# Attention and a gated spatial MLP on one core: part 2 of a written-out order is tied to part 1 on VectorE, ScalarE and the SyncE queue, and the order itself is another

## The chip, the cores and the metric

The kernel runs on one core of one Trainium2 chip. The metric is the device time of one execution in microseconds, and the median of several executions. A core has engines with one instruction queue each: TensorE (PE in the profile, its weight loads PEld), VectorE (DVE), ScalarE (ACT), GpSimd (POOL) and SyncE (SP), which here only issues DMAs. Across engines, an instruction waits on semaphores for what it reads or overwrites.

## The reference

For batch B=4, heads H=4, sequence S=1088, head width D=32 and R=8 features, linear attention with quadratic features, and a gated MLP whose gate mixes positions (w_sg is 1088 x 1088):

```python
def phi(x):
    a = np.einsum('rd,bhsd->bhsr', S1, x)
    b = np.einsum('rd,bhsd->bhsr', S2, x)
    return np.einsum('bhsi,bhsj->bhsij', a, b).reshape(*x.shape[:-1], r * r)
q_p, k_p = phi(q), phi(k)
kv = np.einsum('bhsf,bhsd->bhfd', k_p, v)
z = np.sum(k_p, axis=2)
x = np.einsum('bhsf,bhfd->bhsd', q_p, kv) / (np.einsum('bhsf,bhf->bhs', q_p, z)[..., None] + 1e-06)
...
h = x @ w_in                                  # x: (4, 1088, 128), w_in: (128, 1024)
h = gelu_tanh(h)
u, v = h[..., :512], h[..., 512:]
v_n = (v - mu) / np.sqrt(var + 1e-06) * g_ln  # mean and variance over the last axis
v_s = np.einsum('ts,bsd->btd', w_sg, v_n) + b_sg[None, :, None]
out = x + (u * v_s) @ w_out
```

## The kernel before

Matrices are held as a high word in TensorE's fp32r format and a low word that holds the rest, so that a product is three matmuls (high x high, low x high, high x low). The positions are split into chunks of 420, 420 and 248 columns (CH), the 512 channels of the gate into four blocks of 128. Much of the work by position is done on 9 tiles of 128 positions.

**Tasks and the order.** Nothing is issued while the program is described. `add` and `step` record tasks (an engine, a function, what it reads, writes, takes and frees), 1963 of them. `ORDER` is a list of task numbers, written out, which fixes the order of all work; `plan.run()` replays it and hands out buffers: three banks of PSUM called ps, five buffers gt, three u, two gh, two gl.

**Two parts.** The list is issued in two parts (L1301 on). `staging` names the last tasks that need the pool `stage` (the splitting of the weights w_in and w_out, lines L453 to L471 on VectorE, among them); the first part ends behind the last of these. Then the pool is closed, the pools `x1` and `gate` are opened, and the second part is issued. Each part stands under its own `tc.manual_schedule()`, which keeps the listed order on each engine within the part. Nothing in the program says how the two parts stand to each other on an engine, apart from the dependencies of data and buffers.

**What stands around the cut**, at about 65 us:
- `unit` (L744 to L748): u of one block and chunk, three matmuls into a bank of ps (L746, L747, L748); ScalarE's gelu (L752) frees the bank.
- The first product with w_sg of batch 0 is accumulated in banks that are called `ps`, `po` and `pz` (L680, L1241, L1243). `evac` (L762 on VectorE) adds the bias and writes gt, and the bank is free. `gate` multiplies by u (L776), splits into words (L777, L778), and three matmuls L783 to L785 multiply by w_out.
- `combine` (L865 to L895): makes differences of blocks of w_sg, with which later products take fewer matmuls, in eight rounds. A round loads pieces of w_sg (L879, L881: tmp<-in_w), subtracts on VectorE (L884 to L887), splits (L889, L890 on ScalarE; L891, L892 on VectorE) and stores to DRAM (L894: td<-tmp). The next round's loads overwrite tmp, so they wait for the stores. `combine` also copies words of w_sg as they are (L868: td<-w_h, L870: td<-w_l); the low words of w_sg are made on GpSimd (L700).
- `attention` (L905 to L1042) of the next batch: its scores of q are formed chunk by chunk (L956, L957 words of q, three matmuls L961 to L963), spread by a round trip through DRAM (`fill`, L969 to L975, two loads), multiplied and split (L978 to L980), and multiplied with kv (L987 to L989).
- In the first 25 us the attention of batch 0: products L605 on VectorE of the two halves of the features, L565 to L567 the division, then the transposes L574 on TensorE.

The products of batch 3 (`group` L831 to L833, `tail` L842 and L843, words L806 and L807) run the same way behind 300 us.

Of the kernel before, what the change touches and what calls it, by code (L numbers as in the profile page):

```python
# [20 lines left out]
SP = NT * P  # L21
# [170 lines left out]
def tile_kernel(ctx: ExitStack, tc: tile.TileContext, qd, kd, vd, sd, wd, bd, wind, gd, woutd, identd, outd):  # L192
# [1121 lines left out]
    with tc.manual_schedule():  # L1314
        for i in seq[cut:]:
            issue(plan.tasks[i])
# [36 lines left out]
```

## Time and profile before

| | |
|---|---|
| median of 3 timed runs | 337.05 us (336.94 to 337.54) |
| the profiled execution | 336.07 us |
| its span, first to last instruction | 333.9 us |
| TensorE busy (matmuls), weight loads | 325.9 us (98%), 313.9 us (94%) |
| VectorE busy, 595 instructions | 268.1 us (80%) |
| ScalarE busy, 525 instructions | 219.9 us (66%) |
| GpSimd busy | 55.3 us (17%) |
| granted TensorE clock, mean | 1.000 |

The profile shows one execution. A busy time is the time in which an engine carried out at least one instruction; matmuls overlap each other in the rows, so how long one holds TensorE is read from the distance between the starts of successive ones. The remainder between the span and the time of the execution lies around the first and last instruction.

### The profile page before, as it was taken

What the parts mean: (1) busy time and instruction counts of PE and PEld (TensorE: products, weight loads), DVE (VectorE), ACT (ScalarE), POOL (GpSimd) and SP (SyncE); (2) the same over time, 40 slices, a digit from 0 to 9 for tenths busy, and PEclk for the clock granted to TensorE, in tenths of its full rate; (3) what the DMA queues carried; (4) which work ended last, traced back from release to release, by engine and by line L of the source; (5) the groups of instructions that cost most, each with busy time, mean ns of one, the idle gap of its engine ahead of it and who ended that gap; (6) DMA issues with size and microseconds to landing.
All of it is one profiled execution on the core that took longest, in us unless ns stands there. A gap on an engine that the chain in (4) does not pass through costs nothing.

```text
span 333.9 us, 5891 instructions
## 1 busy us (share of the span) xinstructions
PE 325.9 (98%) x2000; PEld 313.9 (94%) x2000; DVE 268.1 (80%) x595; ACT 219.9 (66%) x525; POOL 55.3 (17%) x130
## 2 busy tenths in 40 slices
PE   7999999979999999999999999999999999999995
PEld 7998899969999999999999999999999999999995
DVE  3898989889986798997985588898964697589394
ACT  6578972646999886636789793746799953342240
POOL 2696781000004300000003300000004400000000
PEclk9999999999999999999999999999999999999999
DMA  7998244647668777882464428563434037115802
GB/s 237 369 397 297 66 111 143 221 128 186 189 176 271 214 170 202 282 283 82 113 215 161 165 75 219 153 214 113 136 106 174 2 101 258 71 52 157 255 3 70
DMA packets 43855, 57.06 MB, mean 171 GB/s; under 512 B 4209, under 2 KB 41137, under 8 KB 43825
## 3 DMA queue, kind: packets, MB, share of 16 engines
q1 hardware_dynamic: 43680, 56.62, 54.3%
q8 instruction: 16, 0.26, 0.3%
q14 instruction: 15, 0.11, 0.1%
q10 hardware_dynamic: 144, 0.06, 0.1%
HBM read 46.73 MB, written 9.95 MB: 170 GB/s over the span
## 4 chain that ended last, share of the span: by engine, by line
PE 76%; DVE 12%; DMA 4%; ACT 4%; issue 2%; SPq 1%; DVEq 0%; POOL 0%; ACTq 0%; POOLq 0%
PE pz L831 14%; PE pz L832 14%; PE pz L833 14%; PE ps L938 3%; PE po L783 2%; PE po L785 2%; PE po L784 2%; PE pz L842 2%; PE pz L843 2%; DMA tmp<-in_w 2%; PE ps L746 2%; PE ps L747 2%; PE ps L748 2%; PE ps L1020 2%; PE ps L1022 2%
## 5 line engine op out<-in xcount | busy, mean ns | idle before, releaser
L831 PE MATMUL pz<-w_h,ar 128*128 128x420 f32 (+1 forms) x288 | 94.3, 327 | 0.1
L832 PE MATMUL pz<-w_h,ar 128*128 128x420 f32 (+1 forms) x288 | 93.2, 324 | 0.0
L833 PE MATMUL pz<-w_l,ar 128*128 128x420 f32 (+1 forms) x288 | 93.1, 323 | 0.0
L831 PEld LDWEIGHTS pz<-w_h,ar 128*128 128x128 f32 x288 | 54.2, 188 | 1.7 <-DVE gt L762 0.7
L832 PEld LDWEIGHTS pz<-w_h,ar 128*128 128x128 f32 x288 | 54.2, 188 | 0.8
L833 PEld LDWEIGHTS pz<-w_l,ar 128*128 128x128 f32 x288 | 54.2, 188 | 0.6
L806 ACT CAST ar<-vn 128x512 fp32r<-128x512 f32 x40 | 24.5, 617 | 22.1 <-PE pz L833 19.4
L777 ACT CAST gh<-gt 128x420 fp32r<-128x420 f32 (+1 forms) x47 | 23.1, 494 | 17.0 <-DVE gt L776 13.0
L752 ACT ACTIVATE u<-ps 128x420 f32<-128x420 f32 (+1 forms) x48 | 22.4, 468 | 15.5 <-DVE gt L776 6.7
L778 DVE TENSOR_TENSOR gl<-gt,gh 128x420 fp32r<-128x420 f32 (+1 forms) x47 | 24.7, 531 | 6.5 <-ACT gh L777 6.3
L807 DVE TENSOR_TENSOR ar<-vn,ar 128x512 fp32r<-128x512 f32 x40 | 27.2, 685 | 0.8 <-ACT ar L806 0.6
L320 ACT ACTIVATE vn<-vn,st 128x512 f32<-128x512 f32 x33 | 25.9, 811 | 1.4 <-POOL st L314 1.4
L776 DVE TENSOR_TENSOR gt<-gt,u 128x420 f32<-128x420 f32 (+1 forms) x47 | 24.7, 529 | 0.2
L762 DVE SCALAR_TENSOR_TENSOR gt<-pz,g_col,b_bc 128x420 f32<-128x420 f32 (+1 forms) x31 | 17.7, 572 | 6.5 <-PE pz L843 4.2
L700 POOL TENSOR_TENSOR w_l<-w_f,w_h 128x420 fp32r<-128x420 f32 (+1 forms) x21 | 21.6, 1055 | 3.2 <-DVE sp_wi_e L457 2.8
L1032 ACT ACTIVATE kp<-vn,st 128x512 bf16<-128x512 f32 x27 | 19.5, 722 | 0.3
L746 PE MATMUL ps<-x_h,win_h 128*128 128x420 f32 (+1 forms) x48 | 16.1, 335 | 2.1 <-DVE gt L762 2.1
L303 POOL TENSOR_TENSOR st<-st 128x4 f32<-128x4 f32 (+2 forms) x8 | 2.4, 302 | 93.2 <-DVE st L285 93.2
L1029 ACT ACTIVATE vn<-ps 128x512 f32<-128x512 f32 x27 | 15.9, 590 | 1.4 <-PE ps L1022 1.3
L747 PE MATMUL ps<-x_h,win_l 128*128 128x420 f32 (+1 forms) x48 | 15.7, 328 | 0.0
L748 PE MATMUL ps<-x_l,win_h 128*128 128x420 f32 (+1 forms) x48 | 15.7, 327 | 0.0
L783 PE MATMUL po<-gh,wout_h 128*128 128x420 f32 (+1 forms) x47 | 15.6, 333 | 0.0
(303 smaller groups left out, 821.0 us busy)
## 6 DMA issues: line engine op xcount, KB each, us to landing
w_l<-td SPq DMA_DIRECT2D x52, 210.0 KB
w_h<-td SPq DMA_DIRECT2D x26, 420.0 KB
td<-tmp SPq DMA_DIRECT2D x16, 315.0 KB
w_f<-in_w SPq DMA_DIRECT2D x9, 544.0 KB
eb<-dq SPq DMA_DIRECT2D x12, 182.0 KB
ea<-dq SPq DMA_DIRECT2D x12, 182.0 KB
vn<-in_k SPq DMA_DIRECT2D x3, 576.0 KB
tmp<-in_w SPq DMA_DIRECT2D x16, 105.0 KB
```

Source lines behind the costliest of these rows:

```text
L320: A.activation(self.vn(t), self.vn(t), AF.Identity, bias=self.nm[:, t : t + 1], scale=self.rs[:, t : t + 1])
L746: mm(o, lhsT=win_h[:, ws], rhs=xh[:, cs], start=True, stop=False)
L747: mm(o, lhsT=win_l[:, ws], rhs=xh[:, cs], start=False, stop=False)
L752: add("A", 0.02 + ap(cw), lambda: A.activation(utt[plan.got[u]][:, :cw], ps(k)[:, :cw], AF.Gelu_apprx_tanh), r=[k], take={u: "u"}, free=[k ...
L776: add("V", dv(cw), lambda: V.tensor_mul(gt(k)[:, :cw], gt(k)[:, :cw], utt[plan.got[u]][:, :cw]), r=[u], w=[k], free=[u], port=1)
L777: add("A", ac(cw), lambda: A.copy(ght[plan.got[h]][:, :cw], gt(k)[:, :cw]), r=[k], take={h: "gh"})
L778: add("V", dv(cw), lambda: V.tensor_sub(glt[plan.got[l]][:, :cw], gt(k)[:, :cw], f32(ght[plan.got[h]][:, :cw])), r=[h, k], take={l: "gl"}, ...
L806: add("A", ac(n), lambda: A.copy(dst[:, 0], q()), r=r, w=[key])
L807: add("V", dv(n), lambda: V.tensor_sub(dst[:, 1], q(), f32(dst[:, 0])), r=r, w=[key], port=1)
L831: mm(o, lhsT=ar[e][:, 0, t], rhs=wh, start=first, stop=False, skip_group_check=True)
L832: mm(o, lhsT=ar[e][:, 1, t], rhs=wh, start=False, stop=False, skip_group_check=True)
L833: mm(o, lhsT=ar[e][:, 0, t], rhs=wl, start=False, stop=last, skip_group_check=True)
```

## The change

Three edits. The list `ORDER` is another one (the same tasks; 164 lines of numbers in the difference, of which the first pair is shown). `fill` hands back its two loads as a tuple; what it issues is the same. And `issue` remembers, while part 1 is issued, the last instruction of VectorE, of ScalarE and of the SyncE queue; in part 2, the first instruction of each of the three gets a dependency on it, of the kind that only the scheduler sees (NoSync, SCHED_ONLY: no semaphore, no instruction).

```diff
 ORDER = [
-    1, 2, 3, 4, 5, 11, 12, 6, 13, 14, 15, 16, 17, 18, 7, 50, 0, 51, 42, 8, 49, 48, 43, 9,
+    1, 2, 3, 4, 5, 11, 12, 6, 13, 14, 15, 16, 17, 18, 7, 45, 49, 8, 48, 0, 42, 46, 9, 51,
...
                 def fill(cw=cw, ci=ci, i=i, e=e):
                     o = here(e)[:, :, :cw]
-                    for p in range(2):
-                        if i:
-                            load(o[:, p], dq[ci][32 + 16 * p : 48 + 16 * p, :cw].unsqueeze(0).broadcast_to([R, 16, cw]))
-                        else:
-                            load(o[:, p], dq[ci][16 * p : 16 * p + 16, :cw].unsqueeze(1).broadcast_to([16, R, cw]))
+                    if i:
+                        return tuple(load(o[:, p], dq[ci][32 + 16 * p : 48 + 16 * p, :cw].unsqueeze(0).broadcast_to([R, 16, cw])) for p in range(2))
+                    return tuple(load(o[:, p], dq[ci][16 * p : 16 * p + 16, :cw].unsqueeze(1).broadcast_to([16, R, cw])) for p in range(2))
...
-    def issue(t):
+    last = {}
+
+    def issue(t, tie=False):
         ins = t["f"]()
+        if t["eng"] in ("V", "A", "SP"):
+            x = ins[0] if isinstance(ins, tuple) else ins
+            if tie and t["eng"] in last:
+                tc.add_manual_dep(x.ins, last.pop(t["eng"]).ins.name, mybir.DependencyInfo(mybir.DependencyClass.NoSync, mybir.DependencyReason.SCHED_ONLY), reason="order")
+            elif not tie:
+                last[t["eng"]] = ins[-1] if isinstance(ins, tuple) else ins
...
     with tc.manual_schedule():
         for i in seq[cut:]:
-            issue(plan.tasks[i])
+            issue(plan.tasks[i], True)
```

Behind `fill` the line numbers of the changed kernel are two lower, so L980 of before is L978 of after, and L995 is L993.

How the instructions stand is shown at three places, all on VectorE. The first is the end of part 1, at 65 to 72 us of the trace. The names sp_wo_ and wout belong to the splitting of w_out, which is part 1; tmp is combine's buffer; ar the words of the normalized v; gt the results of the evacuations; eb and qtl belong to the attention of batch 1. Before:

```order
L458 TENSOR_SCALAR sp_wo_g<-sp_wo_t 128x512
L884 TENSOR_TENSOR tmp<-tmp 128x210
L885 TENSOR_TENSOR tmp<-tmp 128x210
L807 TENSOR_TENSOR ar_92<-vn,ar_92 128x512
L470 TENSOR_TENSOR sp_wo_t<-sp_wo_t,wout_h 128x512
L459 SCALAR_TENSOR_TENSOR sp_wo_e<-sp_wo_e,sp_wo_g 128x512
L995 STREAM_TRANSPOSE r_521<-r_519 128x384
L471 TENSOR_TENSOR wout_l<-sp_wo_t,sp_wo_e 128x512
L998 TENSOR_SCALAR dr<-r_521 128x12
L999 RECIPROCAL dr<-dr 128x12
L886 TENSOR_TENSOR tmp<-tmp 128x210
L762 SCALAR_TENSOR_TENSOR gt_893<-ps_116,g_col,b_bc 128x248
```

After:

```order
L458 TENSOR_SCALAR sp_wo_g<-sp_wo_t 128x512
L978 TENSOR_TENSOR eb<-ea,r_839 128x2x364
L470 TENSOR_TENSOR sp_wo_t<-sp_wo_t,wout_h 128x512
L459 SCALAR_TENSOR_TENSOR sp_wo_e<-sp_wo_e,sp_wo_g 128x512
L957 TENSOR_TENSOR qtl<-qld,qth 128x364
L471 TENSOR_TENSOR wout_l<-sp_wo_t,sp_wo_e 128x512
L807 TENSOR_TENSOR ar_92<-vn,ar_92 128x512
L993 STREAM_TRANSPOSE r_707<-r_705 128x384
L762 SCALAR_TENSOR_TENSOR gt_893<-po_123,g_col,b_bc 128x248
L762 SCALAR_TENSOR_TENSOR gt_894<-pz_119,g_col,b_bc 128x420
L884 TENSOR_TENSOR tmp<-tmp 128x210
L762 SCALAR_TENSOR_TENSOR gt_895<-ps_118,g_col,b_bc 128x248
```

L884 and L885, operations of part 2, stood ahead of L807, L470, L459, L995 and L471 of part 1; they stand behind these now, and L884 behind two evacuations L762. The evacuation that ends the first piece (of 128 x 248, from a bank ps) is the one that ends the second. L980 (now L978) and the query's low word L957 (now L955), which stood ahead of L458, now stand behind it. The bank of that evacuation is used again on TensorE by a matmul L746: between the bank's last product and that matmul stood nine other matmuls, and now twenty.

The second place is in part 1, at 15 to 21 us: the attention of batch 0 and the splitting of w_in (sp_wi_). The names po, ps and pz are banks of PSUM. Before:

```order
L526 TENSOR_TENSOR sg_kvx<-pz_120,mask 128x2x32 x2
L528 TENSOR_TENSOR sg_kvx<-pz_120,mask 128x2 x2
L605 TENSOR_TENSOR vn<-po_122,ea 128x384
L459 SCALAR_TENSOR_TENSOR sp_wi_e<-sp_wi_e,sp_wi_g 128x512
L470 TENSOR_TENSOR sp_wi_t<-sp_wi_t,win_h 128x512
L565 TENSOR_SCALAR den_0_349<-pz_119 128x12
L566 RECIPROCAL den_0_349<-den_0_349 128x12
L567 TENSOR_TENSOR r_104<-pz_119,den_0_349 128x384
L605 TENSOR_TENSOR vn<-po_122,eb 128x384
L605 TENSOR_TENSOR vn<-ps_118,ea 128x384
```

After:

```order
L605 TENSOR_TENSOR vn<-pz_119,eb 128x384
L458 TENSOR_SCALAR sp_wi_g<-sp_wi_t 128x512
L605 TENSOR_TENSOR vn<-po_122,ea 128x384
L526 TENSOR_TENSOR sg_kvx<-pz_120,mask 128x2x32 x2
L528 TENSOR_TENSOR sg_kvx<-pz_120,mask 128x2 x2
L459 SCALAR_TENSOR_TENSOR sp_wi_e<-sp_wi_e,sp_wi_g 128x512
L605 TENSOR_TENSOR vn<-ps_118,ea 128x384
L470 TENSOR_TENSOR sp_wi_t<-sp_wi_t,win_h 128x512
L565 TENSOR_SCALAR den_0_352<-pz_119 128x12
L566 RECIPROCAL den_0_352<-den_0_352 128x12
L567 TENSOR_TENSOR r_104<-pz_119,den_0_352 128x384
L605 TENSOR_TENSOR vn<-po_122,eb 128x384
```

Ahead of L565 to L567 (the division, whose result r the transposes read) now stands an L605 (vn<-ps,ea) that stood behind them; and the L605 of pz, which in the old list stood ahead of all of the splitting of w_in, now stands in the midst of it.

The third place is in part 2, at 301 to 307 us, in the products of the last batch. Before:

```order
L762 SCALAR_TENSOR_TENSOR gt_894<-pz_119,g_col,b_bc 128x420
L762 SCALAR_TENSOR_TENSOR gt_897<-pz_120,ng_col,b_bc 128x420
L807 TENSOR_TENSOR ar_93<-vn,ar_93 128x512
L1080 SCALAR_TENSOR_TENSOR vn<-tmp,vn 128x4x128
L807 TENSOR_TENSOR ar_90<-vn,ar_90 128x512
L1065 TENSOR_TENSOR tmp<-vn 128x512
L1086 TENSOR_TENSOR tmp<-tmp,vn 128x128
L1063 TENSOR_TENSOR rs<-vn,rs 64x256
L776 TENSOR_TENSOR gt_895<-gt_895,u_900 128x420
L1063 TENSOR_TENSOR rs<-tmp,rs 64x256
L762 SCALAR_TENSOR_TENSOR gt_893<-pz_119,g_col,b_bc 128x420
L807 TENSOR_TENSOR ar_91<-vn,ar_91 128x512
```

After:

```order
L762 SCALAR_TENSOR_TENSOR gt_897<-pz_119,g_col,b_bc 128x420
L762 SCALAR_TENSOR_TENSOR gt_894<-pz_120,ng_col,b_bc 128x420
L776 TENSOR_TENSOR gt_896<-gt_896,u_900 128x248
L778 TENSOR_TENSOR gl_904<-gt_895,gh_901 128x420
L762 SCALAR_TENSOR_TENSOR gt_895<-pz_119,g_col,b_bc 128x420
L807 TENSOR_TENSOR ar_90<-vn,ar_90 128x512
```

Between an evacuation with the negative gains (ng_col) and the next from the bank pz_119 stood nine operations; now there are two, and what stood there (the words L807, the combinations L1080, L1065, L1086, L1063) stands elsewhere.

## Rows read from the trace of the kernel before

**Rows 1.** Table of stretches: busy us and instructions by engine, granted clock, DMA.

```profile
64.00:72.00 8.00, 6.15 (x38) 5.76 (x37) 5.51 (x15) 3.00 (x8) 0.00 (x0) 1.00 0.57 147
72.00:80.00 8.00, 7.74 (x41) 7.29 (x42) 7.93 (x17) 6.50 (x16) 0.00 (x0) 1.00 0.55 149
96.00:304.00 208.00, 208.00 (x1278) 202.54 (x1277) 165.55 (x352) 143.98 (x351) 19.42 (x68) 1.00 0.52 159
```

**Rows 2.** Timeline of TensorE at 70 us: start, duration, line, tiles, idle before.

```profile
69.61 0.35 PE L1241 MATMUL pz<-w_l,rs 128*128 128x420 f32 x1
69.80 0.36 PE L680 MATMUL po<-w_l,rs 128*128 128x420 f32 x1
72.26 0.46 PE L746 MATMUL ps<-x_h,win_h 128*128 128x420 f32 x1 [2.11 <-DVE gt L762]
72.56 0.35 PE L747 MATMUL ps<-x_h,win_l 128*128 128x420 f32 x1
```

**Rows 3.** Timeline of VectorE at the end of part 1.

```profile
63.20 0.90 DVE L980 TENSOR_TENSOR eb<-ea,r 128x728 fp32r<-128x728 f32 x1
...
64.32 0.53 DVE L957 TENSOR_TENSOR qtl<-qld,qth 128x364 fp32r<-128x364 f32 x1
64.77 0.41 DVE L458 TENSOR_SCALAR sp_wo_g<-sp_wo_t 128x512 int32<-128x512 int32 x1
67.60 0.38 DVE L884 TENSOR_TENSOR tmp<-tmp 128x210 f32<-128x210 f32 x1 [2.42 <-DMA tmp<-in_w]
...
68.91 0.68 DVE L470 TENSOR_TENSOR sp_wo_t<-sp_wo_t,wout_h 128x512 f32<-128x512 f32 x1
...
70.11 0.57 DVE L995 STREAM_TRANSPOSE r<-r 128x384 f32<-128x384 f32 x1
...
71.75 0.46 DVE L762 SCALAR_TENSOR_TENSOR gt<-ps,g_col,b_bc 128x248 f32<-128x248 f32 x1
```

**Rows 4.** Chain of waits, 58 to 84 us: start, duration, what.

```profile
64.86 2.65 DMA tmp<-in_w
...
73.71 3.09 DMA td<-tmp
...
77.23 3.59 DMA tmp<-in_w
```

**Rows 5.** Timeline of TensorE at 91 us.

```profile
91.25 0.28 PE L832 MATMUL pz<-w_h,ar 128*128 128x248 f32 x1
91.36 0.28 PE L833 MATMUL pz<-w_l,ar 128*128 128x248 f32 x1
91.77 0.43 PE L987 MATMUL ps<-r,kp 128*128 128x360 f32 x1
```

**Rows 6.** Timeline of VectorE at 91 us.

```profile
90.74 0.90 DVE L980 TENSOR_TENSOR eb<-ea,r 128x720 fp32r<-128x720 f32 x1
```

**Rows 7.** Timeline of TensorE at 306 us.

```profile
306.39 0.36 PE L843 MATMUL pz<-w_l,rs 128*128 128x420 f32 x1
306.90 0.46 PE L831 MATMUL pz<-w_h,ar 128*128 128x420 f32 x1
```

**Rows 8.** Timeline of VectorE at 306 us.

```profile
306.19 0.66 DVE L762 SCALAR_TENSOR_TENSOR gt<-pz,g_col,b_bc 128x420 f32<-128x420 f32 x1
```

**Rows 9.** Timeline of VectorE at 19 us.

```profile
19.11 0.56 DVE L567 TENSOR_TENSOR r<-pz,den 128x384 f32<-128x384 f32 x1
...
20.05 0.55 DVE L605 TENSOR_TENSOR vn<-ps,ea 128x384 f32<-128x384 f32 x1
```

**Rows 10.** Timeline of TensorE at 20 us.

```profile
20.06 0.83 PE L574 MATMUL ps<-sg_ident,r 128*128 128x128 f32 x6
```

**Rows 11.** Timeline of the SyncE queue, 36 to 48 us.

```profile
39.07 5.74 SPq L894 DMA_DIRECT2D td<-tmp  x2
...
47.25 0.37 SPq L879 DMA_DIRECT2D tmp<-in_w  x1
```

**Rows 12.** Timeline of GpSimd, 34 to 43 us.

```profile
38.75 3.16 POOL L700 TENSOR_TENSOR w_l<-w_f,w_h 128x420 fp32r<-128x420 f32 x3
```

162 rows, old and new, of the table ORDER are left out of this document.

## The prediction, made before the changed kernel ran

> **What bounds the kernel now.** I read the table of stretches first, the rows of TensorE where it stands still second, and then the engine that it waits for. Between 96 and 304 us TensorE is busy 208.00 of 208 us [rows 1]: in that part another order can win nothing by removing waits, it can only add some. Between 64 and 72 us it is busy 6.15 of 8 us at a granted clock of 1.00, and VectorE only 5.51, although VectorE has 7.93 of 8 us of work in the next stretch [rows 1]. So both wait there, at a time when one of them has no work to spare. What TensorE waits for stands in its rows: L746, a matmul that needs a free bank of PSUM, starts at 72.26, after 2.11 us of idle time, and its releaser is the evacuation L762 on VectorE [rows 2]. The matmul ahead of it started at 69.80. A matmul of this width holds TensorE for 0.19 us (69.61 to 69.80 in the same group), so its turn was at 69.99: the loss is 2.27 us.
>
> VectorE's rows tell why the evacuation is late. It runs from 71.75 to 72.21, as the last of a queue; VectorE itself stood still for 2.42 us ahead of L884, which waited for the transfer tmp<-in_w [rows 3]. In the chain of waits that transfer runs from 64.86 to 67.51 [rows 4]. L884 belongs to combine, so it is work of the second part; five operations of the first part (L807, L470, L459, L995, L471) stand behind it on VectorE, and so does the evacuation. The first fence of the change shows it: two operations of part 2, L884 and L885, were placed ahead of the end of part 1.
>
> **The change, step by step.** It adds no instruction and no semaphore; on each engine the count of instructions is as before. All its effect is order.
>
> *The place at 70 us.* In the new list L884 and L885 stand behind the whole of part 1, and behind two evacuations besides. What is the time of the evacuation that frees the bank? Successive operations of VectorE overlap by 0.08 us (L470 and L459 stand from 68.91 to 70.11, 0.60 each, where a row shows 0.68 [rows 3]), so I count each as its duration less 0.08. Ahead of L458, two operations have gone to places behind it: a subtraction of 728 columns (0.90 in its row) and the query's low word (0.53) [rows 3], together 1.27. L458 ended at 65.18, so it ends at about 63.91. Behind it come, by the same rows: the subtraction 0.82, L470 and L459 1.20, the query's word 0.45, L471 and L807, of the same width as L470, 1.20, the transpose 0.49: 68.07. Then the evacuation of 248 columns 0.38, one of 420 columns 0.58 [rows 8], L884 0.30 and the evacuation in question, 0.46: it ends at about 69.8. If it came in its old place on TensorE, the matmul would want the bank at 69.99. It comes later: nine matmuls stood between the last product into that bank and the next use of it, and now there are twenty, so the next use is some two microseconds after that. The transfer of tmp is no obstacle: it is issued at about the old time, 64.9, and lands by 67.5, while L884 is reached at 69.0. So the wait goes, with the 0.11 us that the following matmul loses (72.26 to 72.56 is 0.30 for 0.19 [rows 2]): **-2.4 us**. What is late next there is the evacuation of 420 columns, whose bank is wanted again ten matmuls after its last product; by the sums it has about 0.7 us to spare.
>
> *The place at 91 us.* TensorE starts L987 0.41 us after a matmul of a width that holds it 0.11 (91.25 to 91.36) [rows 5]; it waited for VectorE's L980, which ended at 91.64 [rows 6]. In the new list more than ten other matmuls stand ahead of L987, two microseconds: **-0.3**.
>
> *The place at 306 us.* The matmul at 306.90 starts 0.51 us after one that holds TensorE 0.19 [rows 7]; an evacuation on VectorE is late, 306.19 to 306.85 [rows 8], with nine other operations between it and the evacuation ahead of it. In the new list there are two (third fence). I take **-0.3**, the whole stall; if another operation is late instead, nothing.
>
> *What the new list loses.* In the first 22 us (second fence) one product L605 now stands ahead of L567 that stood behind it, and another, which stood ahead of the splitting of w_in, now stands within it; each takes 0.55 [rows 9]. L567 ended at 19.67, and the transposes on TensorE that read it began at 20.06 [rows 10], so 0.39 us was to spare and up to 2 x 0.47 is added: a loss of at most 0.55. Some of it may be covered by gaps of VectorE in the same stretch; I take the middle, **+0.3**. In the remaining list, where TensorE has no waits to lose, any place at which an operation is reordered may wait once; three small ones of the kind of [rows 5, 7], 0.3 each, would be 0.9, none would be 0. I take **+0.3**.
>
> The sum is -2.4 - 0.3 - 0.3 + 0.3 + 0.3 = **-2.4 us**. The profiled execution took 336.07 us, 2.17 more than its span of 333.9; the span becomes 331.5 and that execution 333.7. The median of the timed runs is 0.98 above the profiled one, so I forecast **334.6 us**.
>
> **The rivals.**
>
> *The wait moves to the next round of combine.* Its round trip is L891, the store, and the load for the next L884. In the trace it is 3.09 us of store, 0.43 us between them and 3.59 us of load, 7.1 in all [rows 4]. In the new list VectorE has 7.1 us of other work between the two, where it had 7.7. So there is nothing to spare: if the transfers are as slow again it waits by a tenth, and if they come a microsecond later, with more other traffic in the same stretch, VectorE stands still for that time, and the evacuations behind it give about 1.1 us back to the stall: 335.7. For it speaks that two loads of one kind differ by 0.94 us (2.65 and 3.59 [rows 4]); against it, that the chance of meeting the traffic is no larger than before. The Trainium skill, "DMA: Bandwidth & Descriptors", section "Anatomy of one DMA — SWDGE (gpsimd) path", gives 2.0 us and the bytes divided by 436,000 per us for a transfer; for 315 KB and 210 KB that is 2.74 and 2.49, an estimate, so a round trip of 5.6 us with the 0.43 between them, and this rival would not exist. The rows show longer ones, 3.09 and 3.59, and they decide.
>
> *Slower: the SyncE queue stops early.* Two copies td<-w_l (L870), which the old order issued late, stand on the new queue directly ahead of combine's first store L894. They need GpSimd's L700, of which three run one behind the other from 38.75 to 41.91 [rows 12]; the store was issued at 39.07 and the loads behind it at 47.25 [rows 11]. If the copies wait for the last one, the store starts some 3 us later; it lands 3.1 us after, at about 45.5, ahead of 47.25. With the stores' own 1.7 us of slack behind that (45.5 to 47.25), it decides from about 4.7 us of delay on: then every round of combine is late and VectorE stands in front of L884 with evacuations behind it. At a delay of 8.2 us, which is eight pieces of L700 (1.05 each) in place of three, 3.5 us are lost: 338.1.
>
> *No change.* VectorE has 7.93 us of work in 8 behind the place [rows 1]; if the new list has as many close places between 20 and 100 us as the old one, each costing 0.3 to 0.5, six of them eat the gain: 336.8. Against it: VectorE's idle time of 2.42 us goes, whatever the order is.
>
> *More.* None of the losses comes, and the small waits between 24 and 64 us go too: 3.0 to 3.6 us, 333.8.
>
> That the change doesn't do what it says can be left out: the order of instructions shows the two operations in their new place.
>
> **How the numbers follow.** Of a change within 0.2% (0.67 us) a measurement of this kernel can tell nothing. Chances: the forecast 0.60, the next round 0.14, more 0.10, no change 0.09, slower 0.07. Faster is the first three: 0.84; the same 0.09; slower 0.07. The forecast's own spread is 334.0 to 335.5 (losses of 0 to 1.5 us). The range leaves out the slower case and the no-change case and holds the others, 333.4 (the largest gain) to 336.3 (the next round with most of the losses).
>
> **What would show it.** Right: between 64 and 72 us TensorE is busy nearly 8 us and VectorE 7.5 or more; no idle time of VectorE ahead of L884's first operation of the second part, and no row of TensorE near 70 us with over 0.5 us of idle time behind L762. At 20 us the transposes start at 20.1 to 20.6 without a shift elsewhere. The next round: VectorE idle ahead of L884 between 74 and 80 us. The slower case: SyncE's first store issued after 43 us. The prediction is wrong if TensorE's lost time shows up in many small waits in stretches where it has none now, above all between 96 and 304 us.

## The result, and the profile after

The changed kernel takes 333.25 us in the median (332.40 to 334.14, 4 runs) against 337.3 us for the kernel before in the same session (336.94 to 339.21); the ratio is 0.987, with an interval of 0.982 to 0.992, so 4.4 us are gone, with an interval of 2.9 to 6.0 (the two medians lie 4.05 apart). The forecast was 334.6, from 333.4 to 336.3: the sign is right, the gain is larger than forecast, and the time lies just below the range. The profiled execution took 334.14 us with a span of 332.4, which is 1.9 us less than the profiled execution before. So the two traces show less than the medians do, and where the rest lies is what the experiments are about.

The table of stretches after, the lines that answer to [rows 1]:

```profile
64.00:72.00 8.00, 8.00 (x50) 7.69 (x49) 7.85 (x18) 5.01 (x12) 0.00 (x0) 1.00 0.71 189
72.00:80.00 8.00, 8.00 (x44) 7.70 (x43) 7.95 (x16) 5.79 (x14) 0.00 (x0) 1.00 0.60 161
96.00:304.00 208.00, 207.78 (x1268) 201.67 (x1267) 167.00 (x353) 142.33 (x349) 17.42 (x68) 1.00 0.51 156
```

Between 64 and 72 us TensorE is busy 8.00 of 8 us where it was 6.15, VectorE 7.85 where it was 5.51. Between 96 and 304 us TensorE now loses 0.22 us of 208, where it lost nothing; in a second execution, after_again (below), it loses nothing there either.

The timeline of VectorE after, at the place of [rows 3] (L978 is the L980 of before):

```profile
64.82 0.42 DVE L458 TENSOR_SCALAR sp_wo_g<-sp_wo_t 128x512 int32<-128x512 int32 x1
65.16 0.91 DVE L978 TENSOR_TENSOR eb<-ea,r 128x728 fp32r<-128x728 f32 x1
...
68.24 0.69 DVE L807 TENSOR_TENSOR ar<-vn,ar 128x512 fp32r<-128x512 f32 x1
...
69.53 0.43 DVE L762 SCALAR_TENSOR_TENSOR gt<-po,g_col,b_bc 128x248 f32<-128x248 f32 x1
69.89 0.64 DVE L762 SCALAR_TENSOR_TENSOR gt<-pz,g_col,b_bc 128x420 f32<-128x420 f32 x1
70.45 0.36 DVE L884 TENSOR_TENSOR tmp<-tmp 128x210 f32<-128x210 f32 x1
70.73 0.48 DVE L762 SCALAR_TENSOR_TENSOR gt<-ps,g_col,b_bc 128x248 f32<-128x248 f32 x1
```

L884 comes at 70.45 without any idle time ahead of it, and the evacuation that frees the bank is the one at 70.73. Its bank is taken again by the last of these matmuls, the timeline of TensorE after:

```profile
69.53 0.47 PE L746 MATMUL ps<-x_h,win_h 128*128 128x420 f32 x1
69.84 0.36 PE L747 MATMUL ps<-x_h,win_l 128*128 128x420 f32 x1
...
74.28 0.28 PE L746 MATMUL ps<-x_h,win_h 128*128 128x248 f32 x1
```

The matmul comes at 74.28, 3.1 us after the evacuation has ended (71.21). The wait of 2.11 us of [rows 2] is gone; 0.12 us at 69.53 to 69.84 (0.31 for 0.19) is all that is left of it here. At 91 and at 306 us no matmul starts more than 0.1 us late any more, where [rows 5] and [rows 7] showed 0.30 and 0.32.

What came in their place, the waits of TensorE behind the start, as the table of waits of the profile after gives them (in us, times, longest):

```profile
PE po L1181 <- DVE gt L1184: 0.4, 1, 0.4
PE po L682 <- ACT rs L663: 0.2, 1, 0.2
```

The last products of the kernel (L1181) now wait for a VectorE operation between their halves, 0.4 us; and the timeline of TensorE has two places of 0.3 us, of which this is the later:

```profile
128.16 0.35 PE L748 MATMUL ps<-x_l,win_h 128*128 128x420 f32 x1
128.65 0.46 PE L831 MATMUL pz<-w_h,ar 128*128 128x420 f32 x1
```

L831 starts 0.49 us after a matmul that holds TensorE 0.19: an evacuation on VectorE (128.13 to 128.60) is late. In after_again the wait of L1181 is there again, 0.4 us, but neither of the two places of 0.3 us: L831 starts 0.10 us late there, at 127.79.

Two predicted steps can be read directly. At the start, VectorE and TensorE, to be held against [rows 9, 10]:

```profile
19.95 0.56 DVE L567 TENSOR_TENSOR r<-pz,den 128x384 f32<-128x384 f32 x1
```

```profile
20.70 0.83 PE L574 MATMUL ps<-sg_ident,r 128*128 128x128 f32 x6
```

L567 ends at 20.51 where it ended at 19.67; the transposes start at 20.70 and don't wait, because TensorE itself comes later in this execution (it waited 0.7 us for the load of k at 4 us). In a second execution of the changed kernel, after_again, whose start is like that of before, its timeline of TensorE shows the loss:

```profile
16.51 0.34 PE L592 MATMUL po<-ar,ar 128*128 128x384 f32 x1
17.41 1.55 PE L558 MATMUL pz<-sg_kvx,vn 128*128 128x66 f32 x12 [0.57 <-DVE sg_kvx L528]
```

L558 waits 0.57 us for VectorE's L528 and starts 0.73 us later than its turn (0.17 behind 16.51); L528 is late because two L605 now stand ahead of it next to L458: the one of the bank pz, which stood ahead of the whole splitting of w_in, and the one of the bank po, which stood behind L528 (second place of the change). And the SyncE queue of the first execution after, against [rows 11]:

```profile
41.81 0.81 SPq L870 DMA_DIRECT2D td<-w_l  x2
42.71 0.41 SPq L894 DMA_DIRECT2D td<-tmp  x1
...
50.02 0.54 SPq L881 DMA_DIRECT2D tmp<-in_w  x1
```

The copies L870 do hold the queue until GpSimd has finished L700: the first store goes out at 42.71 instead of 39.07 and the next loads at 50.02 instead of 47.25. This is the mechanism of the slower rival, with a delay of 3.6 us, of which 2.8 reach the loads. VectorE doesn't wait for them: the L884 behind them starts at 56.38 without idle time ahead of it, and TensorE doesn't wait for any of it. (VectorE ends L458 at 65.24, where the sum of the prediction had 63.91. It was late before it came there: L454 of the same splitting starts at 61.37, and before the change at 59.44. Why was not followed back.)

### The profile page after: what moved, and what is told of

Its sections match the earlier page's. It is cut to its first block, busy times and chain, and to the rows that moved or that the text cites. A ratio compares the mean times of both kernels' runs of the same rounds, so it can differ in the third digit from the quotient of the medians.

```text
span 332.4 us, 5902 instructions
## 1 busy us (share of the span) xinstructions
PE 326.5 (98%) x2000; PEld 315.2 (95%) x2000; DVE 270.1 (81%) x595; ACT 218.3 (66%) x525; POOL 53.5 (16%) x130
## 4 chain that ended last, share of the span: by engine, by line
PE 74%; ACT 7%; DVE 7%; DMA 6%; POOL 3%; issue 2%; SPq 1%; DVEq 0%; ACTq 0%; POOLq 0%
PE pz L831 13%; PE pz L832 13%; PE pz L833 13%; DMA tmp<-in_w 4%; PE ps L746 2%; PE ps L747 2%; PE ps L748 2%; PE po L783 2%; PE po L785 2%; PE po L784 2%; PE pz L842 2%; PE pz L843 2%; PE pz L516 1%; PE po L680 1%; PE ps L1019 1%
## 5 line engine op out<-in xcount | busy, mean ns | idle before, releaser
L831 PE MATMUL pz<-w_h,ar 128*128 128x420 f32 (+1 forms) x288 | 94.2, 327 | 0.1
L831 PEld LDWEIGHTS pz<-w_h,ar 128*128 128x128 f32 x288 | 54.1, 188 | 1.9 <-DVE gt L762 0.5
L807 DVE TENSOR_TENSOR ar<-vn,ar 128x512 fp32r<-128x512 f32 x40 | 27.2, 685 | 2.3 <-ACT ar L806 2.1
L762 DVE SCALAR_TENSOR_TENSOR gt<-pz,g_col,b_bc 128x420 f32<-128x420 f32 (+1 forms) x31 | 17.7, 572 | 7.4 <-PE pz L843 3.7
L700 POOL TENSOR_TENSOR w_l<-w_f,w_h 128x420 fp32r<-128x420 f32 (+1 forms) x21 | 21.6, 1057 | 2.6 <-ACT w_h L653 2.2
L746 PE MATMUL ps<-x_h,win_h 128*128 128x420 f32 (+1 forms) x48 | 16.0, 333 | 0.0
L257 DVE TENSOR_TENSOR kp<-ps,kb 128x256 f32<-128x256 f32 x27 | 11.1, 421 | 5.8 <-ACT kb L928 4.6
```

The source lines that it names most:

```text
L746: mm(o, lhsT=win_h[:, ws], rhs=xh[:, cs], start=True, stop=False)
L807: add("V", dv(n), lambda: V.tensor_sub(dst[:, 1], q(), f32(dst[:, 0])), r=r, w=[key], port=1)
L831: mm(o, lhsT=ar[e][:, 0, t], rhs=wh, start=first, stop=False, skip_group_check=True)
```

## The experiments

"Old list" is ORDER of before, "new list" that of after; "tied" means with the dependency across the two parts. Medians in us; "fastest" is the lowest time of the kernel.

| kernel | median | fastest | runs |
|---|---|---|---|
| before, in three sessions | 337.11, 337.29, 337.26 | 335.68, 335.49, 335.89 | 22, 29, 17 |
| before_again | 337.13 | 335.97 | 12 |
| old_tied_asp: old list, tied on ScalarE and the queue | 337.36 | 335.69 | 12 |
| old_tied: old list, tied | 333.62 | 333.27 | 11 |
| old_tied_v: old list, tied on VectorE alone | 333.46 | 333.20 | 6 |
| tied_filled: old_tied and useless matmuls in the gap | 335.42 | 335.15 | 12 |
| after_again: the changed kernel | 333.54 | 333.35 | 6 |
| new_untied: new list, not tied | 333.20 | 332.15 | 6 |
| new_hoisted: new list, L884 and L885 put ahead again | 336.12 | 335.64 | 12 |
| start_v: the changed kernel, v loaded ahead of q | 335.85 | 333.90 | 12 |

**How far executions lie apart.** Both kernels, unchanged, again.

before_again: 

> The kernel before, unchanged, a second time: how far executions of one program lie apart, and a second trace of it. Theory A (the profiled execution of before was a fast one, 1 us under its median, and the forecast was built on it): the times spread over 1.5 to 2.5 us and the median comes out 336.9 to 337.5; the first 10 us differ from the first trace by 0.3 to 0.7 us. Theory B (the first trace is typical): within 0.5 us of 336.1.

after_again: 

> The changed kernel, unchanged, a second time. Theory A: the median comes out 333 to 333.5, 1 us below its first profiled execution of 334.14, so that the two profiled executions understate the difference (1.9 us) and the medians show it (about 3.9). Theory B (the profiled executions are right and the medians are off by chance): 334.2 and a difference of 2 to 2.5 us.

The kernel before spreads from 335.97 to 339.42, the changed one from 333.35 to 334.17. The ratio of the second measurement is 0.989, from 0.986 to 0.992, that is 3.7 us; the difference of the medians in the same session is 3.6. So the medians are no accident, and the first profiled execution of before, 336.07, was quicker than most of its kind. But theory A had the place wrong: the two traces of before stand within 0.02 us of each other ahead of the wait (the matmul there starts at 69.80 and 69.78), and the wait in the second is what it was in the first, 2.3 us with the slow matmul behind it.

**The tie alone, and the list alone.**

```diff
 ORDER = [
-    (the new list)
+    (the old list, in old_tied)
...
-            issue(plan.tasks[i], True)
+            issue(plan.tasks[i])
```

The first pair of lines is old_tied, the second pair, with the new list, is new_untied (there `issue` is that of before altogether).

old_tied: 

> The old list with the tie: L884 and L885 go back behind part 1 on VectorE, all else is as before. Forecast's theory (the gain is the wait at 70 us): the TensorE idle time of 2.1 us goes and the time falls by 2.0 to 2.4 us. Rival (the list brings it: only with the other places changed does the wait go): the evacuation is then late behind other operations and under 1 us is won, with the wait showing up within 5 us behind.

new_untied: 

> The new list without the tie. On VectorE and ScalarE it gives the same order as the changed kernel; on the SyncE queue two loads of combine (L879, L881) go ahead of part 1's dq<-ab and a store. Forecast's theory: within 0.5 us of the changed kernel, since VectorE's order carries the gain. Rival (the tie carries it, through the queue): the loads wait for combine's words, dq<-ab behind them is late, and 1 us or more is lost against the changed kernel.

The tie alone brings 3.5 us (0.9905, from 0.987 to 0.994): more than the 2.0 to 2.4 that were expected of it, though the fastest executions lie 2.4 apart (335.68 and 333.27). What the list brings beyond it, 0.1 us in after_again and 0.4 in new_untied, does not stand clear of the spread. Without the tie the new list is as fast as with it (333.20 and 333.54): its own order on VectorE leaves no operation that goes ahead, and the two loads that do go ahead on the queue cost nothing. So either edit would have done alone.

Which engine's tie it is, by the condition in `issue`:

```diff
-        if t["eng"] in ("V", "A", "SP"):
+        if t["eng"] in ("V",):
```

and ("A", "SP") in the other.

old_tied_v: 

> The old list with the tie on VectorE alone; a second execution of that order to look at. Theory P (the wait at 70 us is the whole of it, on VectorE): the time is that of the old list with all three ties, 333.4 to 334.0, TensorE's idle time of 2.1 us at 70 us is gone, and no other stretch behind 24 us changes by over 0.3 us. Rival Q (ScalarE's or the queue's tie has a part): it stays 0.5 us or more above.

old_tied_asp: 

> The old list with the tie on ScalarE and the SyncE queue and none on VectorE: L884 and L885 stay ahead of part 1. Theory P: as the kernel before, median 336.7 to 337.4, and the profiled execution has the wait at 70 us again, 2.2 us or, if it differs between executions, another size that goes with its time. Rival Q: 336.5 or less.

It is VectorE's alone: 333.46 and 337.36, both within what theory P gave, and old_tied_asp has the wait at 70 us again (2.12 us). The timeline of VectorE in old_tied_v:

```profile
64.49 0.42 DVE L458 TENSOR_SCALAR sp_wo_g<-sp_wo_t 128x512 int32<-128x512 int32 x1
...
67.12 0.65 DVE L471 TENSOR_TENSOR wout_l<-sp_wo_t,sp_wo_e 128x512 fp32r<-128x512 f32 x1
67.69 0.37 DVE L884 TENSOR_TENSOR tmp<-tmp 128x210 f32<-128x210 f32 x1
...
68.97 0.47 DVE L762 SCALAR_TENSOR_TENSOR gt<-ps,g_col,b_bc 128x248 f32<-128x248 f32 x1
```

L884 starts right behind L471, with no idle time, and the evacuation ends at 69.44 instead of 72.21. The matmul that needs the bank comes on its turn, the timeline of TensorE in old_tied_v:

```profile
69.52 0.35 PE L680 MATMUL po<-w_l,rs 128*128 128x420 f32 x1
69.71 0.35 PE L746 MATMUL ps<-x_h,win_h 128*128 128x420 f32 x1
```

**The reverse.** L884, L885 and their loads moved in the new list to behind L458:

```diff
-    ..., 210, 323, 463, ..., 631, ..., 629, ..., 632, ..., 630, ..., 633, ...
+    ..., 631, 629, 630, 210, 632, 633, 323, 463, ...
```

new_hoisted: 

> The new list with L884 and L885 put back by hand directly behind L458 (their loads too go ahead on the queue, as in the new list without the tie, which cost nothing). Theory P: VectorE waits about 2.2 us for the load at 65 us, the evacuations behind it are late by 2.5 us with 0.4 to 0.7 us to spare, and TensorE loses 1.8 to 2.4 us: 335.2 to 336. Rival R (the new list has room enough there by itself): under 0.7 us, 334.1 or less.

Most of the gain is lost again, 2.6 of 3.6 us by the medians of the two sessions (336.12 against 333.54), 0.1 more than theory P gave. The timelines of VectorE and TensorE in new_hoisted:

```profile
64.40 0.42 DVE L458 TENSOR_SCALAR sp_wo_g<-sp_wo_t 128x512 int32<-128x512 int32 x1
67.00 0.38 DVE L884 TENSOR_TENSOR tmp<-tmp 128x210 f32<-128x210 f32 x1 [2.19 <-DMA tmp<-in_w]
...
67.71 0.91 DVE L978 TENSOR_TENSOR eb<-ea,r 128x728 fp32r<-128x728 f32 x1
```
```profile
66.59 0.32 PE L986 MATMUL ps<-r,kp 128*128 128x364 f32 x1
68.67 0.44 PE L987 MATMUL ps<-eb,kp 128*128 128x364 f32 x1 [1.76 <-DVE eb L978]
```

VectorE waits 2.19 us, as expected, and TensorE 1.76. But TensorE waits for L978, which stands nearer behind L884 in this list, and not for the evacuation, as theory P had it. The new list has no room for such a wait either.

**Why the medians show more than the wait.** In the old list the tie wins 2.3 to 2.4 us between the fastest executions, and 3.5 to 3.8 between the medians. To tell whether the rest belongs to the end of the execution or to the wait, the gap was filled: in old_tied, ahead of the matmul that had waited,

```diff
+            for _ in range(12 if (b, db, ci) == (0, 2, 0) else 0):
+                mm(o, lhsT=win_h[:, ws], rhs=xh[:, cs], start=True, stop=True)
             mm(o, lhsT=win_h[:, ws], rhs=xh[:, cs], start=True, stop=False)
```

tied_filled: 

> The old list tied, with 12 useless matmuls of 420 columns ahead of the matmul that waited at 70 us: TensorE is kept busy there for as long (12 x 0.19 = 2.3 us) as it stood idle. The medians of the tied and the untied old list lie 3.4 to 3.8 us apart, the traces and the fastest executions only 2.3. Theory E (the rest comes at the end: an execution that ends at 334 instead of 331 us meets something there that delays the last store): 336.7 to 337.3, with executions spread up to 339 as in the kernel before. Theory W (the rest is in the wait itself, which differs between executions): 335.7 to 336.1, with three quarters of the executions within 0.7 us of the fastest.

The timeline of TensorE in tied_filled:

```profile
70.03 2.46 PE L747 MATMUL ps<-x_h,win_h 128*128 128x420 f32 x12
72.33 0.35 PE L748 MATMUL ps<-x_h,win_h 128*128 128x420 f32 x1
```

With 2.30 us of useless work (70.03 to 72.33) in place of the 2.27 that the matmul of before was late, the kernel takes 335.42, and ten of its twelve runs lie between 335.15 and 335.83: 1.8 us less than the kernel before in the same session, at the same length of the gap. Theory E falls: the kernel ends nearly as late as the quickest executions of the untied one (the fastest are 335.15 and 335.89), and its runs lie close together. The time is also below the 335.7 to 336.1 of theory W, of which the small spread came true. Here, standing idle was dearer than working for nothing. Three more traces of the kernel before tell why.

before_look_a: 

> The kernel before, one more execution to look at. Of three traces of it (or of its order) the wait at 70 us was 2.2 to 2.3 us in each, while the time from TensorE's last matmul to the end of the span was 4.5, 4.9 and 6.2 us, with times of 336.1, 336.5 and 337.6. Theory E: the wait is 2.2 to 2.3 us again, and the time is 331.5 to 332 and the stretch from the last matmul's start to the end, within 0.6 us. Theory W: the wait differs by as much as the time does.

before_look_b: 

> As before_look_a, another execution: theory E, a wait of 2.2 to 2.3 us at 70 us, and what the time differs by lies behind the last matmul or in the first 24 us; theory W, in the wait.

before_look_c: 

> As before_look_a, another execution: theory E, a wait of 2.2 to 2.3 us at 70 us, and what the time differs by lies behind the last matmul or in the first 24 us; theory W, in the wait.

They took 339.39, 337.52 and 335.98 us. The idle time at 70 us is nearly the same in all, 2.12, 2.19 and 1.98 us, so theory W, as it was put, falls too: the wait differs by 0.2 us, the times by 3.4. What differs comes right behind it (and, in before_look_a, ahead of it as well); the table of stretches of before_look_b (the number ahead of the last two is the granted clock):

```profile
70.00:72.00 2.00, 0.03 (x1) 0.00 (x0) 1.97 (x7) 0.68 (x2) 0.00 (x0) 1.00 0.40 106
72.00:73.00 1.00, 0.79 (x2) 0.77 (x3) 1.00 (x4) 1.00 (x3) 0.00 (x0) 0.58 0.00 0
73.00:74.00 1.00, 1.00 (x4) 0.96 (x4) 1.00 (x3) 0.89 (x3) 0.00 (x0) 0.50 0.00 0
...
75.00:76.00 1.00, 1.00 (x5) 0.96 (x5) 0.57 (x3) 0.79 (x3) 0.00 (x0) 0.71 0.89 211
76.00:77.00 1.00, 1.00 (x7) 0.99 (x6) 1.00 (x3) 0.20 (x1) 0.00 (x0) 1.00 0.87 280
```

and its timeline of TensorE:

```profile
72.22 0.72 PE L746 MATMUL ps<-x_h,win_h 128*128 128x420 f32 x1 [2.19 <-DVE gt L762]
72.73 0.55 PE L747 MATMUL ps<-x_h,win_l 128*128 128x420 f32 x1
73.08 0.55 PE L748 MATMUL ps<-x_l,win_h 128*128 128x420 f32 x1
...
75.67 0.35 PE L746 MATMUL ps<-x_h,win_h 128*128 128x420 f32 x1
75.86 0.35 PE L747 MATMUL ps<-x_h,win_l 128*128 128x420 f32 x1
```

TensorE stood idle from 70 to 72.2 us, and then its granted clock is 0.50, the level of 1.2 GHz, until about 75.6: a matmul of 420 columns holds it for 0.35 us (72.73 to 73.08) in place of 0.19 (75.67 to 75.86). Seven matmuls of 420 and three of 364 columns, from 72.22 to 75.67, took 3.45 us; at the distances of the full clock (0.19 and 0.165) they take 1.83, and the first has 0.11 more in any case, so the low clock cost 1.5 us there. In before_look_c the clock stays at 1.00, and its timeline of TensorE at the same place is:

```profile
72.04 0.46 PE L746 MATMUL ps<-x_h,win_h 128*128 128x420 f32 x1 [1.98 <-DVE gt L762]
72.33 0.36 PE L747 MATMUL ps<-x_h,win_l 128*128 128x420 f32 x1
```

Ahead of the gap the two executions stand 0.03 us apart, behind the fall before_look_b is 1.7 us later (0.2 from the longer wait), and behind 92 us 1.2: the place at 91 us, where before_look_c waits, gives 0.4 back. The spans differ by 1.0 us; the other 0.5 of the 1.54 us between the two times lies outside the span. Neither theory had the fall. In before_look_a the clock falls at the same place, between 75 and 79 us (0.56, 0.50, 0.50 and 0.73 in the four stretches of 1 us); it also came to the gap 2.2 us later than the first trace of before, at 72.03, mostly from waits in its first 24 us. As in before_look_c, the clock stays at 1.00 at this place in the two traces of the kernel before and in old_tied_asp: two of six traces of the old order show the fall, and the trace of new_hoisted, with 1.76 us of idle time, does not; nor does any of the seven traces without the wait, at this place.

Every execution, traced or not, has its mean granted clock on record. A fall like that in before_look_b brings the mean to 0.995, in that execution too, and no execution shows a mean between 0.995 and 0.997. So the executions can be counted:

| executions | all | mean granted clock 0.995 or lower |
|---|---|---|
| old list with the wait: before in three sessions, before_again, old_tied_asp | 92 | 50 |
| without the wait: old_tied, old_tied_v, tied_filled, after, after_again, new_untied | 45 | 2 |
| new_hoisted | 12 | 3 |

The mean doesn't say where the clock fell. But the tied kernels with the old list start as before does, so most of the 50 falls belong to the wait. Of the 68 executions of before in the three sessions, the 39 with the low mean have a median of 337.82 us, the 29 others 336.40, and all together 337.24; the 17 of old_tied and old_tied_v have 333.61. Of the 3.6 us between the last two, the falls make 0.8 (337.24 to 336.40) and the length of the wait 2.4 (2.27, and 0.11 for the matmul behind it); 0.4 are left unexplained.

**A wait at the start.** The other place where TensorE stands idle for long is at 7 to 9 us, in most traces for the loads of v. In start_v the two `yield` lines of v stand ahead of those of q:

```diff
         yield "k1", (1.7,), lambda: load(k0[:, 3 * P :], kd[0, :, 3 * P :])
+        yield "v0", (0.88,), lambda: load(vx()[:, :NT], vd[0, :, 0])
+        yield "v1", (0.75,), lambda: load(vx()[:, NT + 1 :], vd[0, :, 1])
         yield "q0", (0.5,), lambda: load_q(0)
```

start_v: 

> The changed kernel with the two loads of v issued ahead of the four of q, all else the same. In the traces so far TensorE waits 0.4 to 2.7 us for v at 7 to 9 us. Theory S (executions differ by that wait): it goes, the time falls by 0.3 to 0.8 us and no execution is over 334.5. Rival T (the loads share the same transfers' rate; q is then late in its place): the same time within 0.3 us.

Both theories missed: 335.85, 2.3 us slower than the changed kernel in the median. On ScalarE the words of q (L583) stand ahead of a copy that the features of k need (L533). In the timeline of ScalarE L583 now starts at 7.78, after 2.27 us of waiting for q, and L533 at 8.44; TensorE's L516 starts at 9.55 after 1.9 us of idle time. The profile puts that wait down to GpSimd's L584, the low word of q, which reads what L583 writes; either way it is q that is late. (The profiled execution of old_tied, its slowest at 337.35, lost as much by chance: 2.5 us of idle time ahead of 9.46 and 0.15 more for v behind it, and then a granted clock of 0.50 from 11 to 14 us.) In start_v, too, the clock falls behind the wait, as its table of stretches shows:

```profile
10.00:11.00 1.00, 1.00 (x8) 1.00 (x7) 1.00 (x3) 0.66 (x3) 1.00 (x2) 0.59 1.03 363
11.00:12.00 1.00, 1.00 (x7) 1.00 (x6) 1.00 (x5) 0.00 (x0) 1.00 (x2) 0.50 0.94 347
12.00:13.00 1.00, 1.00 (x6) 1.00 (x5) 1.00 (x4) 0.00 (x0) 0.90 (x1) 0.50 1.02 383
...
14.00:16.00 2.00, 2.00 (x18) 2.00 (x17) 1.97 (x5) 2.00 (x4) 0.72 (x1) 1.00 1.02 407
```

## Why the prediction was off

- *The wait and its cause*: right. Two operations of part 2 ahead of part 1 on VectorE, their load, the evacuation behind them, and TensorE behind that: old_tied_v takes it away by VectorE's tie alone, new_hoisted brings most of it back (there with L978 in the place of the evacuation).
- *The step that failed* is the last one of the sum: "The median of the timed runs is 0.98 above the profiled one, so I forecast 334.6 us". The sum ahead of it came out in the span: 331.5 forecast, 331.45 in the median of the four executions. On top of the span the forecast put 2.17 + 0.98 us, 3.15 in all, carried over from the old kernel as if the change could not touch them; measured were 1.8 (333.25 less 331.45). The 0.98 was in the main the wait's own price. The term "So the wait goes ... -2.4 us" priced the wait at its length in one execution, in which the granted clock stayed at 1.00. Its length is right (2.0 to 2.2 us of idle time in all six traces that have it). But 39 of 68 executions of before have the low mean clock, and only 1 of 17 of the tied old list; that makes 0.8 us of before's median, and it goes when the wait goes. So in the median the term of the wait is -3.5 (old_tied) to -3.8 (old_tied_v) in place of -2.4. The median of before lies 1.2 to 1.8 us over its fastest run; those of the tied old list lie 0.3 over theirs.
- *The 2.17 us outside the span*, put on the changed kernel unaltered: 1.74 to 1.93 in all 40 executions of kernels with the new list, 2.08 or more in all with the old one, tied or not. So 0.4 us belong to the list, and the prediction had no term for them. What makes them stays open.
- *The list's gains and losses*, -0.3 - 0.3 + 0.3 + 0.3: right in the sum of the times (old_tied to the changed kernel: -0.1), but in part by luck: the spans of the new list are 0.1 to 0.4 us longer than those of the tied old one (medians 331.45, 331.45 and 331.7 against 331.25 and 331.4), and the 0.4 outside the span makes up for it. The places at 91 and 306 us are gone as forecast. The loss in the first 22 us came where TensorE was on time, but by a step that the prediction did not have: 0.73 us in after_again, at L558, which waits for L528, and not at the transposes. It was hidden where TensorE was late. The loss in the remaining list came in the last products, in both executions, and at 113 and 128 us in the first alone.
- *The next round of combine*: did not come. L884 of the next round starts at 80.66 us behind a full VectorE (7.95 of 8 us), without waiting for its load.
- *The slower rival*: its first half came, 3.6 us of delay on the queue against the 4.7 at which it was to decide. The slack that it counted on was not there, since 2.8 us of the delay reached the loads; still VectorE did not wait for them.
- *More*: its size came (3.0 to 3.6 forecast, 3.6 to 4.4 measured), its reason did not. TensorE is busy 39.80 of 40 us between 24 and 64 us, and 39.88 before, so the small waits there did not go.
- *No change*: VectorE came 1.3 us later to the place than the sum had it, and it was no matter, since the matmul that needs the bank was 3.1 us behind the evacuation.

Open are the 0.4 us of the wait's price in the median that neither its length nor the low clock makes up, and why the clock falls in one execution and not in the next. Some executions are long for another reason: in old_tied_asp, at 337.63 us, the clock did not fall at 70 us, and the time lies at the end. The last store was issued at 330.87 and the span ends at 335.5, where in the first trace of before these are 331.07 and 333.9. Whether that belongs to the order at all was not tried.

## What to carry to other kernels

When a program is issued in several scheduled parts, look at the built order of each engine at the seams: an instruction of the next part that slips ahead of the end of the last one brings its own wait with it, and everything behind it in the queue pays. Price a wait on TensorE above its length: the clock may be lower afterwards, and one trace in which it isn't does not show that. Before a sum made on one profiled execution is carried to the median, ask what the difference of the two is made of, and whether the change touches it; the span and the mean granted clock of every execution say more about that than the times.

## What the runs showed of the hardware

TensorE's granted clock fell from 1.00 to 0.50 behind an idle time of 2.1 and 2.2 us in two traces of six, and not in the other four, with the same order on VectorE and 2.0 to 2.1 us of idle time; behind the idle time of 1.9 us at the start it fell in start_v as well. In 50 of 92 executions with the wait the mean granted clock was 0.995 or lower, in 2 of 45 without it, and in 3 of 12 of new_hoisted, whose trace has a wait of 1.76 us and no fall. The Trainium skill, "TensorE: Matmul & The Clock Gate", section "Part 1: The HAM clock gate", says that idle time lets the clock fall to half, and that the gate looks at the engine at times which don't follow the kernel; by that the same idle time would fare differently from execution to execution, as in these rows, but no run here shows the gate itself. By that section's account idle times as short as these would not have let the clock fall; the rows show that they did, and they decide. Twelve matmuls with no use, issued in the idle time, went with a clock of 1.00 in the trace, the table of stretches of tied_filled:

```profile
64.00:72.00 8.00, 8.00 (x50) 7.91 (x49) 7.93 (x20) 4.75 (x11) 0.00 (x0) 1.00 0.55 147
72.00:80.00 8.00, 8.00 (x45) 7.75 (x44) 6.63 (x14) 5.13 (x13) 0.00 (x0) 1.00 0.65 164
```
